# Two score banks lent to the last burst, a last row block in three pieces, and one hash a unit earlier

## The chip, the core and the metric

The kernel runs on one core of one Trainium2 chip. The core has a matrix engine (TensorE; PE in the profile, PEld for its weight loads), VectorE (DVE), ScalarE (ACT), GpSimd (POOL) and a sync engine (SP) that only issues transfers. The metric is the device time of one execution in microseconds, lower is better. A profiled execution gives a span, from the first to the last instruction, and a time that is a little longer.

## What is computed

Hash attention over 4 batches, 8 heads, 768 positions and 64 dimensions, and behind it a feed-forward block with a maximum of three projections. Attention is kept only between positions whose six hash bits agree:

```python
q_bits = (np.einsum('bhsd,dk->bhsk', q, proj) > 0)
k_bits = (np.einsum('bhsd,dk->bhsk', k, proj) > 0)
mask = q_bucket[:, :, :, None] == k_bucket[:, :, None, :]
scores = np.where(mask, scale * q @ k.T, -1e9)
attn = softmax(scores)                  # 768 x 768 for each head
x = (attn @ v) laid out as (3072, 512)
h = np.maximum(np.maximum(x @ w1, x @ w2), x @ w3)   # 3072 x 768
out = h @ w_out                                      # 3072 x 512, float32
```

## The kernel before, in words

**Scores and hash in one matmul.** For each head there is a tile S with the 64 transposed dimensions of q and k in rows 0 to 63 and the hash bits, as plus and minus one half, in the rows below. One matmul over these rows gives the score and the agreement of the bits at once; the exponential's bias takes away what disagreeing bits leave. Heads are handled in pairs for batch 0 and in quads (four heads, numbered 0 to 7) after it. A quad's q and k are loaded by POOL or SP (`load_quad`), transposed on VectorE (`turn`, L200), narrowed to bf16 on POOL (`narrow`, L205), and placed into S by eight SP transfers (`place`, L210). `quad_hash` (L219) makes the bits: sixteen matmuls into a bank, a comparison on VectorE (L222) and four SP transfers into S (L230): first the key's two halves, then the query's. The transfers are sent one unit after the matmuls.

**Units.** Queries are cut into nine chunks: three of 256 queries for batch 0, then six of 384. A unit is one chunk, one head and a part of the keys: its scores (L296, two or three matmuls) go into a score tile of two PSUM banks; ScalarE takes the exponential (L304) into one of 24 buffers. There are 192 units. The score pool holds two such tiles, so four banks of PSUM are its own. In unit u TensorE first computes the scores of unit u + 1, then the jobs listed for that unit (`when`), then one group of FFN work if any stands in the list, then a burst if one is due, then a hash if `hash_at` names one. All engines follow the order in which this Python program writes the instructions; transfers on SP, ACT and POOL each keep their order too.

**Adds and bursts.** From the fourth chunk on VectorE adds the exponentials of a head (L327, L330). When four heads of a chunk are done, a burst follows: `sums` (L351, matmuls with ones), with a chain on VectorE that turns them into reciprocals (L358 to L362), then `values` for side 0 and for side 1 (L373, 24 matmuls each), whose results VectorE scales into x (L380). The 32-column matmuls of a burst and of a hash work in four strips of the array.

**Banks.** The other four PSUM banks are a ring: `bank()` takes the one that has been free longest, `give()` puts it back in the program's order. Hash, sums, values and FFN groups all draw from it, and a group waits until the engine that empties its bank has done so.

**FFN.** For each chunk 18 groups of four matmuls (L406) make the three projections; the first goes to SBUF by ScalarE or VectorE (L411, L413), the other two are merged in by VectorE (L415). Then for each block of 128 rows two items of three matmuls with w_out (L450), a copy on ScalarE (L454) and a transfer to the output (L456). The groups of a chunk join a list two units after its last burst, and about one is taken from the list in each unit. After unit 191 the last three listed groups, the last burst, what is left of chunk 7's list and the whole FFN of chunk 8 follow. The very last block of 128 rows of chunk 8 is special: `last` (L427) computes it in two pieces of 256 columns (L431), copied by ScalarE (L435) and VectorE (L437) and sent from ACT's and SP's queue (L439).

Of the kernel before, what the change touches and what calls it, by code (L numbers as in the profile page):

```python
# [17 lines left out]
def kernel(  # L18
# [73 lines left out]
        return i, bank_tiles[i]  # L92

    def give(i):
        free_banks.append(i)


    nat, t32, t16, s_of, where, v_at = {}, {}, {}, {}, {}, {}
# [240 lines left out]
    def burst(c, i):  # L339
        b, q0, w = chunks[c]  # L340
        held = {}
        rb = []

        def sums(m0, m1):
            if m0 == 0:
                held["s"] = bank()
            sm = held["s"][1]
            bs = [sum_blocks(c, 4 * i + x) for x in range(4)]
            for m in range(len(bs[0])):
                for x in range(4):  # L350
                    nc.tensor.matmul(sm[Q * x : Q * (x + 1), 0:w], ones[:, :], bs[x][m],  # L351
                                     start=(m == 0), stop=(m == len(bs[0]) - 1))
            if m1 == NM:
                ys = ys_pool.tile([P, HALF], FP32, tag="ys", name="ys")
                rr = small.tile([P, HALF // Q], FP32, tag="rr", name="rr")
                n = w // Q
                rb.append(rb_pool.tile([P, HALF], FP32, tag="rb", name="rb"))
                nc.vector.transpose(ys[:, 0:w], sm[:, 0:w])  # L358
                give(held["s"][0])
                nc.vector.tensor_scalar(out=rr[:, 0:n], in0=ys[:, 0:w:Q], scalar1=EPS * S, scalar2=None, op0=AluOp.add)  # L360
                nc.vector.reciprocal(rr[:, 0:n], rr[:, 0:n])
                nc.vector.transpose(rb[0][:, 0:w], rr[:, 0:n].unsqueeze(2).to_broadcast((P, n, Q)))  # L362

        def values(side, m0, m1):
            if m0 == 0:
                held[side] = bank()
            av = held[side][1]
            first = (b, i, side) not in sv_of
            n = w + 1 if first else w
            for m in range(m0, m1):  # L370
                cb = block_of(b, m)
                for x in range(4):
                    nc.tensor.matmul(av[Q * x : Q * (x + 1), 0:n], v_at[2 * b + i][:, x, cb * D + side : (cb + 1) * D : 2],  # L373
                                     weights_of(c, 4 * i + x, m)[:, 0:n], start=(m == 0), stop=(m == NM - 1))
            if m1 == NM:
                if first:
                    sv_of[b, i, side] = small.tile([P, 1], FP32, tag=f"sv{side}", name="sv")
                    nc.vector.tensor_scalar(out=sv_of[b, i, side][:], in0=av[:, w : w + 1], scalar1=EPS, scalar2=None,
                                            op0=AluOp.mult)
                nc.vector.scalar_tensor_tensor(out=xt_of(c)[:, 2 * i + side, 0:w], in0=av[:, 0:w],  # L380
                                               scalar=sv_of[b, i, side][:], in1=rb[0][:, 0:w], op0=AluOp.add, op1=AluOp.mult)
                give(held[side][0])
                if side == 1:
                    for h in range(4 * i, 4 * i + 4):
                        for n in range(parts_of(c)):
                            a = at_of[unit_at[c, h, n]]
                            if b == 0 and i == 1:
                                nc.gpsimd.memset(blocks(at_tiles[a], HALF)[:, :, HALF : HALF + 2], 1.0)
                                at_form[a] = HALF
                            at_free.append(a)  # L390

        return sums, values


    def ffn_groups(c):
        b, q0, w = chunks[c]
        xt = xt_of(c)
        hts, gs, l2 = {}, [], {}
        jobs = [(fb, wi) for fb in range(NFB) for wi in range(3)]
        if c == 0:  # L400
            jobs = [(fb, wi) for wi in range(3) for fb in range(NFB)]
        for fb, wi in jobs:
            def go(fb=fb, wi=wi):
                k_, ps = bank()
                for jc in range(NJC):
                    nc.tensor.matmul(ps[:, 0:w], w_sb[wi][:, jc, fb * P : (fb + 1) * P], xt[:, jc, 0:w],  # L406
                                     start=(jc == 0), stop=(jc == NJC - 1))
                if wi == 0:
                    hts[fb] = h_pool.tile([P, HALF], FP16, tag="ht", name="ht")
                    if w == HALF:  # L410
                        nc.scalar.copy(hts[fb][:, 0:w], ps[:, 0:w])  # L411
                    else:
                        nc.vector.tensor_copy(hts[fb][:, 0:w], ps[:, 0:w])  # L413
                else:
                    nc.vector.tensor_tensor(out=hts[fb][:, 0:w], in0=hts[fb][:, 0:w], in1=ps[:, 0:w], op=AluOp.max)  # L415
                give(k_)
            gs.append(go)
        rows = out[b * S : (b + 1) * S, :].rearrange("(p c) m -> c p m", c=NM)

        def out_rows(tb):  # L420
            if c < NCH - 1:
                return o_pool.tile([P, DM], FP32, tag="osb", name="osb")
            if "end" not in nat:
                nat["end"] = nat_pool.tile([P, 4 * NM * D], FP32, tag="nat", name="nat")
            return nat["end"][:, tb * DM : (tb + 1) * DM]

        def last(part, tb):  # L427
            k_, ps = bank()
            cs = slice(part * DM // 2, (part + 1) * DM // 2)
            for fb in range(NFB):  # L430
                nc.tensor.matmul(ps[:, 0 : DM // 2], hts[fb][:, tb * P : (tb + 1) * P], wout_sb[:, fb, cs],  # L431
                                 start=(fb == 0), stop=(fb == NFB - 1))
            osb = out_rows(tb)
            if part == 0:
                nc.scalar.copy(osb[:, cs], ps[:, 0 : DM // 2])  # L435
            else:
                nc.vector.tensor_copy(osb[:, cs], ps[:, 0 : DM // 2])  # L437
            give(k_)
            (nc.scalar, nc.sync)[part].dma_start(rows[block_of(b, q0 // P + tb)][:, cs], osb[:, cs])  # L439

        def item(tb, part):
            def go2(part, tb=tb):
                if c == NCH - 1 and tb == w // P - 1:
                    last(part, tb)
                    return
                if part == 0:
                    l2[tb] = bank()
                k_, ps = l2[tb]
                for fb in range(part * MH, (part + 1) * MH):
                    nc.tensor.matmul(ps[:, 0:DM], hts[fb][:, tb * P : (tb + 1) * P], wout_sb[:, fb, :],  # L450
                                     start=(fb == 0), stop=(fb == NFB - 1))
                if part == 1:
                    osb = out_rows(tb)
                    nc.scalar.copy(osb[:, 0:DM], ps[:, 0:DM])  # L454
                    give(k_)
                    nc.sync.dma_start(rows[block_of(b, q0 // P + tb)], osb[:, 0:DM])  # L456
            gs.append(lambda: go2(part))

        ntb = w // P
        steps = [(0, 0)]  # L460
        for tb in range(1, ntb):
            steps += [(tb, 0), (tb - 1, 1)]
        steps.append((ntb - 1, 1))
        if c == NCH - 1:
            steps = steps[:-3] + [steps[-2], steps[-3], steps[-1]]
        for tb, part in steps:
            item(tb, part)
        return gs
# [6 lines left out]
    with tc.manual_schedule():  # L475
# [88 lines left out]
        for g in range(2, NQUAD):  # L564
            b2, i2 = divmod(g, 2)
            need = UPB * b2 + 12 * i2
            for n, side in enumerate((1, 0)):
                name = (side, g)
                if g > 3:
                    us = [SPREAD[b2][0] + SPREAD[b2][1] * (8 * i2 + 4 * n + n2) // 4 for n2 in range(4)]  # L570
                    for x in range(4):
                        when(us[0] - 14 + x, load_quad, side, g, (x,), nc.gpsimd)
                else:
                    us = [need - {2: 26, 3: 23}[g] + 4 * n + n2 for n2 in range(4)]
                for n2, u2 in enumerate(us):
                    when(u2, turn, name, n2 // 2, n2 % 2)
                    if n2 % 2:
                        when(u2 + 1, narrow, name, n2 // 2)
                when(us[3] + 3, place, name, range(4))
            hash_at[{2: 32, 3: 48, 4: need - 12}.get(g, need - 9)] = g  # L580
            when({2: 36, 3: 46}.get(g, need - 22), load_v, g)

        ffn, credit = [], 0
# [75 lines left out]
```

## Time and profile before

| what | value |
|---|---|
| median of 3 runs | 268.19 us (267.94 to 268.28) |
| the profiled execution | 268.58 us |
| its span | 266.6 us |
| TensorE busy | 257.9 us, 97% of the span |
| VectorE busy | 208.9 us, 78% |
| ScalarE busy | 177.3 us, 67% |
| GpSimd busy | 69.9 us, 26% |
| granted TensorE clock | full speed throughout |

Rows of the timeline give the start and the length of a run of equal instructions, the engine, the source line, the operation, the tile written and read, the shape and the count; in brackets the idle time before it and who ended it. Matmuls are pipelined, so the length of a row holds the drain of its last matmul, and starts are the better measure. "PEld" is a weight load, "SPq" the issue of a transfer. A row of busy time by stretch gives, for PE, PEld, DVE, ACT and POOL, busy microseconds and instructions, then the granted clock, the share of the 16 DMA engines and the GB/s. Rows of groups end in busy time, mean ns of one, and idle time before.

### The profile page before, as it was taken

The numbers are of one execution on the slowest core, as the hardware profiler recorded it, in microseconds if no ns is written. First come the engines' busy times: TensorE is split into PE (matmuls) and PEld (weight loads), VectorE is DVE, ScalarE is ACT, GpSimd is POOL, SyncE is SP. The second block draws the span as 40 slices with busy tenths as digits, with TensorE's granted clock in tenths as the row PEclk, the third lists the DMA queues.
The fourth block names the chain that finished last, engine by engine and source line by source line (L and its number), as shares of the span: only waits on it lengthen the run. The fifth ranks groups of instructions, "written<-read, shape, count | busy, mean of one in ns | idle before, by whom it ended". The sixth has DMA issues, their size and how long they took to land.

```text
span 266.6 us, 6482 instructions
## 1 busy us (share of the span) xinstructions
PE 257.9 (97%) x2505; PEld 154.4 (58%) x2505; DVE 208.9 (78%) x493; ACT 177.3 (67%) x257; POOL 69.9 (26%) x132
## 2 busy tenths in 40 slices
PE   7899999999799999999999999999999999999995
PEld 4555557885566575555555554555555555554552
DVE  2897685987499999978998997899849785888361
ACT  3596785676758694984869578484895859581322
POOL 3588652355032535240141612011000000000000
PEclk9999999999999999999999999999999999999999
DMA  6977999969703791982054472802030003000303
GB/s 203 316 156 135 230 234 212 245 114 233 185 22 86 159 231 18 234 222 53 4 167 131 56 182 43 204 8 61 15 118 4 0 2 119 2 0 2 118 0 118
DMA packets 20717, 30.95 MB, mean 116 GB/s; under 512 B 2608, under 2 KB 15248, under 8 KB 20688
## 3 DMA queue, kind: packets, MB, share of 16 engines
q0 software_dynamic: 8128, 13.37, 26.6%
q1 hardware_dynamic: 12128, 16.66, 21.8%
q10 hardware_dynamic: 432, 0.52, 0.6%
q8 instruction: 19, 0.31, 0.5%
q14 instruction: 10, 0.08, 0.1%
HBM read 25.17 MB, written 6.29 MB: 118 GB/s over the span
## 4 chain that ended last, share of the span: by engine, by line
PE 84%; DVE 7%; ACT 5%; issue 3%; DVEq 0%; ACTq 0%
PE ms L406 31%; PE sc L296 21%; PE ms L373 11%; PE ms L450 10%; ACT AT L304 4%; PE ms L351 3%; PE ms L219 3%; DVE ht L415 2%; DVE ad L327 1%; PE ms L498 1%; PE ms L122 1%; PE ms L149 1%; DVE T L131 1%; PE ms L169 1%; DVE S L174 1%
## 5 line engine op out<-in xcount | busy, mean ns | idle before, releaser
L304 ACT ACTIVATE AT<-sc 128x768 f16<-128x768 f32 x192 | 152.3, 816 | 62.2 <-PE sc L296 60.7
L406 PE MATMUL ms<-xT,w_sb 128*128 128x384 f16 (+1 forms) x648 | 114.8, 307 | 0.1
L296 PE MATMUL sc<-S 72*128 72x384 bf16 (+1 forms) x432 | 93.6, 308 | 3.3 <-ACT AT L304 1.8
L406 PEld LDWEIGHTS <-w_sb 128*128 128x128 f16 x648 | 62.7, 97 | 35.9 <-issue 0.4
L415 DVE TENSOR_TENSOR ht<-ht,ms 128x384 f16<-128x384 f16 (+1 forms) x108 | 54.3, 504 | 24.4 <-PE ms L406 13.4
L296 PEld LDWEIGHTS <-S 72*128 72x128 bf16 (+1 forms) x432 | 39.4, 98 | 35.7 <-issue 15.5
L205 POOL TENSOR_SCALAR T<-T 128x768 bf16<-128x768 f32 x24 | 22.8, 952 | 95.4 <-issue 50.5
L450 PE MATMUL ms<-wout_sb,ht 128*128 128x512 f16 x138 | 35.5, 378 | 0.0
L373 PE MATMUL ms<-AT,vo 128*32 128x385 f16 (+3 forms) x864 | 35.2, 309 | 0.3 <-DVE ht L415 0.3
L327 DVE TENSOR_TENSOR ad<-ad,AT 128x768 f16<-128x768 f16 x48 | 26.6, 553 | 2.1 <-ACT AT L304 1.3
L373 PEld LDWEIGHTS <-vo 128*32 128x32 f16 x864 | 22.6, 96 | 9.6 <-issue 1.8
L200 DVE STREAM_TRANSPOSE T<-nat 128x384 f32<-128x384 f32 x48 | 27.0, 565 | 0.2 <-DMA nat<-in_q_dram 0.2
L327 DVE TENSOR_TENSOR ad<-AT,AT 128x768 f16<-128x768 f16 x48 | 26.2, 546 | 0.2 <-ACT AT L304 0.2
L411 ACT CAST ht<-ms 128x384 f16<-128x384 f32 x36 | 17.3, 479 | 8.1 <-PE ms L406 8.1
L380 DVE SCALAR_TENSOR_TENSOR xT<-ms,sv,rb 128x384 f16<-128x384 f32 (+1 forms) x36 | 19.8, 567 | 1.4
L450 PEld LDWEIGHTS <-ht 128*128 128x128 f16 x138 | 13.3, 97 | 13.0 <-issue 0.3
L454 ACT COPY osb<-ms 128x512 f32<-128x512 f32 x21 | 12.2, 585 | 8.2 <-PE ms L450 6.3
L330 DVE TENSOR_TENSOR ad<-ad 128x384 f16<-128x384 f16 x32 | 15.5, 484 | 1.1
L136 POOL TENSOR_SCALAR S<-T 64x384 bf16<-64x384 f32 (+1 forms) x23 | 14.2, 617 | 5.0 <-DVE T L131 3.5
L358 DVE STREAM_TRANSPOSE ys<-ms 128x384 f32<-128x384 f32 (+1 forms) x18 | 9.6, 532 | 6.2 <-PE ms L351 6.2
L194 POOL DMA_DIRECT2D nat<-in_q_dram x20 | 11.1, 560 | 0.1
L413 DVE CAST ht<-ms 128x256 f16<-128x256 f32 x18 | 7.4, 413 | 4.0 <-PE ms L406 3.9
(48 smaller groups left out, 123.0 us busy)
## 6 DMA issues: line engine op xcount, KB each, us to landing
out_dram<-osb SPq DMA_DIRECT2D x21, 256.0 KB
S<-T SPq DMA_DIRECT2D x48, 96.0 KB
nat<-in_q_dram POOLq DMA_DIRECT2D x20, 192.0 KB, 6.7
vo<-in_v_dram POOLq DMA_DIRECT2D x8, 384.0 KB, 6.2
nat<-in_k_dram POOLq DMA_DIRECT2D x16, 192.0 KB, 5.7
w_sb<-in_moe_w_dram POOLq DMA_DIRECT2D x3, 768.0 KB, 6.9
nat<-in_k_dram SPq DMA_DIRECT2D x10, 192.0 KB
nat<-in_k_dram SPq DMA_DIRECT2D x3, 384.0 KB
```

Source lines behind the costliest of these rows:

```text
L200: nc.vector.transpose(t32[name][:, u, half * HALF : (half + 1) * HALF], i_)
L205: nc.gpsimd.tensor_scalar(out=t16[name][:, u, :], in0=t32[name][:, u, :], scalar1=RS, scalar2=1.0, op0=AluOp.mult, op1=AluOp.mult)
L296: nc.tensor.matmul(views[j], s_of[kn][0 : D + bits, kx, m * P : (m + 1) * P], s_of[qn][0 : D + bits, qx, q0 : q0 + w], start=True, stop=True)
L304: nc.scalar.activation(t[:, :, 0:w], whole, ActFn.Exp, bias=-SCALE * 0.25 * bits, scale=SCALE)
L327: nc.vector.tensor_tensor(out=sum_of[c, h][:], in0=t[0], in1=t[n], op=AluOp.add)
L330: nc.vector.tensor_tensor(out=t[:, 0, :], in0=t[:, 0, :], in1=t[:, 1, :], op=AluOp.add)
L373: nc.tensor.matmul(av[Q * x : Q * (x + 1), 0:n], v_at[2 * b + i][:, x, cb * D + side : (cb + 1) * D : 2], weights_of(c, 4 * i + x, m)[:, 0 ...
L380: nc.vector.scalar_tensor_tensor(out=xt_of(c)[:, 2 * i + side, 0:w], in0=av[:, 0:w], scalar=sv_of[b, i, side][:], in1=rb[0][:, 0:w], op0=A ...
L406: nc.tensor.matmul(ps[:, 0:w], w_sb[wi][:, jc, fb * P : (fb + 1) * P], xt[:, jc, 0:w], start=(jc == 0), stop=(jc == NJC - 1))
L411: nc.scalar.copy(hts[fb][:, 0:w], ps[:, 0:w])
L415: nc.vector.tensor_tensor(out=hts[fb][:, 0:w], in0=hts[fb][:, 0:w], in1=ps[:, 0:w], op=AluOp.max)
L450: nc.tensor.matmul(ps[:, 0:DM], hts[fb][:, tb * P : (tb + 1) * P], wout_sb[:, fb, :], start=(fb == 0), stop=(fb == NFB - 1))
```

## The change

Three things change.

- In the second burst of the last chunk, `sums` and `values` for side 0 take a tile of the score pool in place of a bank of the ring; `values` for side 1 still takes a bank of the ring. `give` passes over what was not taken from the ring.
- The last block of 128 rows is computed in three pieces of columns, 256, 128 and 128. The first is copied by VectorE and sent from SP's queue, the second by ScalarE from its own queue, the third by VectorE from SP's queue.
- The hash of quad 3 stands at unit 47 in place of 48: ahead of the last burst of chunk 2 in place of behind it.

```diff
     def give(i):
-        free_banks.append(i)
+        if i is not None:
+            free_banks.append(i)
...
+        def own_bank(key):
+            if c == NCH - 1 and i == 1 and key != 1:
+                return None, sc_ps.tile([P, 2, 512], FP32, tag="sc", name="sc")[:, 0, :]
+            return bank()
+
         def sums(m0, m1):
             if m0 == 0:
-                held["s"] = bank()
+                held["s"] = own_bank("s")
...
         def values(side, m0, m1):
             if m0 == 0:
-                held[side] = bank()
+                held[side] = own_bank(side)
...
-        def last(part, tb):
+        def last(tb, cs, use_act):
             k_, ps = bank()
-            cs = slice(part * DM // 2, (part + 1) * DM // 2)
+            n = cs.stop - cs.start
             for fb in range(NFB):
-                nc.tensor.matmul(ps[:, 0 : DM // 2], hts[fb][:, tb * P : (tb + 1) * P], wout_sb[:, fb, cs],
+                nc.tensor.matmul(ps[:, 0:n], hts[fb][:, tb * P : (tb + 1) * P], wout_sb[:, fb, cs],
                                  start=(fb == 0), stop=(fb == NFB - 1))
             osb = out_rows(tb)
-            if part == 0:
-                nc.scalar.copy(osb[:, cs], ps[:, 0 : DM // 2])
+            if use_act:
+                nc.scalar.copy(osb[:, cs], ps[:, 0:n])
             else:
-                nc.vector.tensor_copy(osb[:, cs], ps[:, 0 : DM // 2])
+                nc.vector.tensor_copy(osb[:, cs], ps[:, 0:n])
             give(k_)
-            (nc.scalar, nc.sync)[part].dma_start(rows[block_of(b, q0 // P + tb)][:, cs], osb[:, cs])
+            (nc.scalar if use_act else nc.sync).dma_start(rows[block_of(b, q0 // P + tb)][:, cs], osb[:, cs])
...
-                    last(part, tb)
+                    if part == 0:
+                        last(tb, slice(0, DM // 2), False)
+                    else:
+                        last(tb, slice(DM // 2, 3 * DM // 4), True)
+                        last(tb, slice(3 * DM // 4, DM), False)
                     return
...
-            hash_at[{2: 32, 3: 48, 4: need - 12}.get(g, need - 9)] = g
+            hash_at[{2: 32, 3: 47, 4: need - 12}.get(g, need - 9)] = g
```

## The prediction

> **What bounds the kernel now.** I read the page first, then TensorE's rows in order of time, looking for places where its starts fall out of their pitch, and only there the queues and the other engines.
>
> ```profile
> span 266.6 us, 6482 instructions
> PE 257.9 (97%) x2505; PEld 154.4 (58%) x2505; DVE 208.9 (78%) x493; ACT 177.3 (67%) x257; POOL 69.9 (26%) x132
> ```
>
> TensorE is busy for 97% of the span, so time is to be had only where it stops, and after its last matmul. I found two odd stops after the opening. The first (timeline of TensorE, of SyncE's queue, busy time by stretch, DMA queues from 66 to 71 us):
>
> ```profile
> 68.78 0.48 PE L296 MATMUL sc<-S 72*128 72x384 bf16 x2
> 69.54 0.49 PE L296 MATMUL sc<-S 72*128 72x384 bf16 x2
> 71.95 0.48 PE L296 MATMUL sc<-S 72*128 72x384 bf16 x2 [1.48 <-ACT AT L304]
> ...
> 53.29 6.18 SPq L210 DMA_DIRECT2D S<-T  x8
> 62.08 2.94 SPq L230 DMA_DIRECT2D S<-bits  x4
> 63.63 0.67 SPq L230 DMA_DIRECT2D S<-bits  x1
> ...
> 70.00:71.00 1.00, 0.47 (x5) 0.18 (x2) 1.00 (x3) 0.94 (x2) 0.00 (x0) 1.00 1.01 270
> 71.00:72.00 1.00, 0.05 (x1) 0.08 (x2) 0.03 (x1) 0.00 (x0) 0.00 (x0) 1.00 0.56 213
> ...
> q0 software_dynamic: 250, 0.74, 69.9%
> q1 hardware_dynamic: 318, 0.40, 31.9%
> ```
>
> Scores come every 0.76 us (68.78, 69.54); the next should start at 70.30 and starts at 71.95, so **1.65 us** are lost. ScalarE is named, but in the stretch 71 to 72 it is busy 0.00: it had long been done. Counting scores back to the first of 72 rows and 384 columns (unit 48), the late one is unit 60, the first to read the S tile of quad 3. The last things written into that tile are the hash bits, sent in four transfers at 62.08 to 65.02. Key and query, first halves, are the first and third of them; the third is issued at 63.63, and the wait ends 8.3 us later. In between the DMA engines are full (share 1.01), most of it POOL's loads on queue 0 (69.9% against 31.9% for SyncE's queue 1). So I read the stop as the third transfer of bits coming late. The landing itself has no row; it is inferred.
>
> The second stop is in the last burst, shown below with its terms.
>
> **The change, part by part: the hash.** Quad 3's hash is moved from the end of unit 48, behind the burst of chunk 2, to the end of unit 47, ahead of it. Its 16 matmuls, the copy of the bits and the four transfers move; their number stays.
>
> ```profile
> 48.77 0.49 PE L296 MATMUL sc<-S 70*128 70x256 bf16 x3
> 51.72 0.50 PE L296 MATMUL sc<-S 70*128 70x256 bf16 x3
> ...
> 55.17 0.56 DVE L200 STREAM_TRANSPOSE T<-nat 128x384 f32<-128x384 f32 x1
> 57.10 0.49 PE L296 MATMUL sc<-S 72*128 72x384 bf16 x2
> 59.95 1.46 PE L219 MATMUL ms<-T,pj 128*32 128x384 f32 x16
> 61.35 0.50 PE L296 MATMUL sc<-S 72*128 72x384 bf16 x2
> 61.49 0.56 DVE L222 TENSOR_SCALAR bits<-ms 128x384 bf16<-128x384 f32 x1 [0.28 <-PE ms L219]
> ...
> 99.01 0.49 PE L296 MATMUL sc<-S 72*128 72x384 bf16 x2
> 101.30 0.50 PE L296 MATMUL sc<-S 72*128 72x384 bf16 x2
> ...
> 61.09 1.09 POOL L194 DMA_DIRECT2D nat<-in_k_dram  x2 [0.40 <-issue]
> nat<-in_k_dram POOLq DMA_DIRECT2D x4, 192.0 KB, 6.2
> 74.05 0.57 DVE L200 STREAM_TRANSPOSE T<-nat 128x384 f32<-128x384 f32 x1
> ```
>
> What the move costs TensorE: from scores to scores, less the pitch of 0.76, burst and hash together take 61.35 - 57.10 - 0.76 = 3.49. A burst alone takes 51.72 - 48.77 - 0.76 = 2.19, a hash alone 101.30 - 99.01 - 0.76 = 1.53. Apart they cost 3.72: **+0.23 us**, an entry to and an exit from the 32-column matmuls more.
>
> What it gives: the hash starts at about 57.2 (where unit 49's scores start now, plus the entry) instead of 59.95. Its last input, the transpose of 55.17, is done. The copy follows 61.49 - 59.95 = 1.54 later, from 58.74 to 59.30. SyncE's queue has the eight placements ahead of it until 53.29 + 6.18 = 59.47, so the bits go out from 59.5: 2.6 us earlier, in the same order. TensorE reaches unit 60 at 70.30 + 0.23 = 70.53. The third transfer, if its time in the queue stays, lands at 71.95 - 2.6 = 69.4. The stop goes if 71.95 - 70.53 = 1.42 of the 2.6 come through. The bounds: all of the stop goes, -1.65 + 0.23 = -1.42; nothing comes through, 0 (TensorE then only arrives later at the same landing). I take **-1.42**, because the four transfers stand in one queue behind the same placements, only sooner.
>
> Who is late next: the burst is 1.5 us later, and behind its matmuls wait POOL's memsets and, queued after those, the two key loads of 61.09 and four query loads. The key loads land 6.2 after issue, the last near 67.8, then near 69.3; VectorE transposes them first at 74.05, then 72.6. It holds. Chunk 2's x is later by as much, but its FFN groups stand behind all of chunk 1's in a list that gives about one a unit. In VectorE's queue the copy moves ahead of the burst's chain, which then has a matmul burst to wait for anyway. ScalarE starves in two short pauses instead of one.
>
> **The last burst.** Sums and the first value matmuls get a score bank each instead of a bank of the four.
>
> ```profile
> 229.93 0.35 PE L351 MATMUL ms<-ad,ones 128*32 128x384 f16 x4
> 230.11 2.12 PE L373 MATMUL ms<-AT,vo 128*32 128x384 f16 x48
> ...
> 239.22 0.81 ACT L304 ACTIVATE AT<-sc 128x768 f16<-128x768 f32 x1 [0.17 <-PE sc L296]
> 241.78 1.21 DVE L415 TENSOR_TENSOR ht<-ht,ms 128x384 f16<-128x384 f16 x2
> 242.38 0.35 PE L351 MATMUL ms<-ad,ones 128*32 128x384 f16 x4
> 243.04 2.13 PE L373 MATMUL ms<-AT,vo 128*32 128x384 f16 x48 [0.31 <-DVE ht L415]
> 244.67 1.17 DVE L380 SCALAR_TENSOR_TENSOR xT<-ms,sv,rb 128x384 f16<-128x384 f32 x2
> 247.70 4.55 PE L406 MATMUL ms<-xT,w_sb 128*128 128x384 f16 x27
> ```
>
> In the burst before, values follow sums by 0.18 us; here by 0.66, because the values' bank is emptied by the second of the two L415 that end at 242.99. With a score bank they follow by 0.18: **-0.48 us**. The new wait is on the exponential that last read the score bank; that ends at 240.03, before the sums' adds. The second values still take a ring bank, the one of the first L415, free before they start. VectorE's chain of the burst is not shortened: x is finished at 245.84 as now. That was hidden under projections until 247.70 and, with TensorE 0.48 earlier, still has 1.4 us of cover. Had those projections not stood between, the gain would be nothing. It cannot be a loss, since a bank is only added; 0 and -0.6 are its bounds.
>
> **The last row block.** Its 512 columns come as 256, 128 and 128 instead of 256 and 256; copies on VectorE, ScalarE, VectorE.
>
> ```profile
> 261.99 1.47 PE L431 MATMUL ms<-wout_sb,ht 128*128 128x256 f16 x12
> L431 PEld LDWEIGHTS <-ht 128*128 128x128 f16 x12 | 1.2, 98 | 0.3
> 9.09 1.48 PE L122 MATMUL ms<-iden,nat 128*128 128x128 f32 x12
> L122 PEld LDWEIGHTS ms<-iden,nat 128*128 128x128 f32 x48 | 6.0, 148 | 0.4 <-issue 0.2
> ...
> 263.50 0.42 DVE L437 COPY nat<-ms 128x256 f32<-128x256 f32 x1 [3.27 <-PE ms L431]
> 263.96 0.33 SPq L439 DMA_DIRECT2D out_dram<-nat  x1
> ...
> 264.80:265.20 0.40, 0.00 (x0) 0.00 (x0) 0.00 (x0) 0.00 (x0) 0.00 (x0) 1.00 0.94 318
> 265.20:265.60 0.40, 0.00 (x0) 0.00 (x0) 0.00 (x0) 0.00 (x0) 0.00 (x0) 1.00 0.07 21
> ```
>
> Twelve matmuls of 256 columns took 1.47 with the last one's drain, a pitch of about 0.11; the last six become twelve of 128. If columns set the pitch, it is half, and nothing changes; if each has to sit out its weight load of 98 ns, twelve cost 1.18 instead of 0.66, +0.52. The nearest row has the same 128 by 128 shape in f32: pitch about 0.11 while its loads show 148 ns, so a pitch may run 0.04 or so below the load's length. I take 0.06 to 0.07, **+0.14**. The last copy: 384 columns took 0.56 (the bits), 256 took 0.42, so 128 take 0.28: **-0.14**. Issue is unchanged (the first copy and its transfer moved to VectorE and SyncE come before, off the end; ScalarE's middle piece has its own queue). The last transfer is half as large, but the DMA engines run full (0.94) until 265.2 on the same bytes, now in more rows: **-0.10**, between -0.2 and 0. Sum -0.10, bounds -0.2 and +0.4.
>
> A sentence apart: the Trainium skill, "TensorE: Matmul & The Clock Gate", section "Back-to-back issue gap", gives about 81 ns per pair of load and matmul at 128 columns; by that, an estimate, the twelve take 0.97, +0.32, and the total would be 0.18 worse than mine. No row of this kernel shows the f16 case.
>
> **Sum.** -1.42 - 0.48 - 0.10 = -2.00. The profiled execution took 268.58, 0.39 above the median of 268.19 (span 266.6): 266.58 there, **266.2** as a median.
>
> **The rivals.**
> - *The bits come no earlier.* If the transfers are held not by when they are issued but by POOL's loads, they land when those thin out, near 71 us, as now. For it: queue 0's 69.9%. Against: queue 1 moved 0.40 MB in the same time. Then -0.48 - 0.10: 267.6. Chance 0.14. (The Trainium skill, "DMA: Bandwidth & Descriptors", "Queues, rings and completion order", says that each engine takes turns between queues packet by packet; by it queue 1 is slowed but served, and the shares above agree.)
> - *VectorE paces the stretch after.* If it was catching up behind the stop, the 1.42 comes back as bank waits: 267.6. Against: it also idled in the stop (0.03 busy from 71 to 72), so both start the stretch drained either way. Chance 0.04.
> - *Narrow matmuls pay their whole load.* +0.52 - 0.14 instead of -0.10: 266.7. Chance 0.08.
> - *Slower: the last small rows.* B and C write 512-byte rows. If such rows travelled like the bits (768-byte rows, 8.3 us from issue to the end of the wait) instead of the 1.3 us in which the last piece's data now moves (263.96 to about 265.3), up to 7 us would be added; the sign turns once it is over 2.0. Against: the bits shared the engines with loads, and at the end there are none. At its full price 273. Chance 0.04.
>
> My forecast as it stands has 0.70, with its own range 265.8 to 266.6. From 265.7 to 267.8 all but the slower case and some of the edges is held. A difference of 0.2% (0.54 us) is about what can be told from none here. The cases at 267.6 lie on that bound and are halved: faster 0.87, same 0.09, slower 0.04.
>
> **What would show it.** Right: the L219 group of quad 3 near 57.2 and its bits issued near 59.5; unit 60's scores 0.76 after unit 59's; about 0.23 more between unit 48 and unit 50; L373 0.18 after L351 in the last burst; twelve narrow matmuls at a pitch of 60 to 70 ns; the last copy 0.28. Wrong: a stop at unit 60 that still ends near 72, new bank waits between 80 and 110 us, or a last transfer that ends later after its issue than now.

## The result, and the profile after

The changed kernel takes 267.14 us (median of 5 runs, 267.10 to 267.48) against 268.28 for the kernel before beside it (267.94 to 268.88): ratio 0.9958, 95% interval 0.9943 to 0.9973. That is faster by 1.1 us, a little over half of the 2.0 that I forecast. It lies outside my forecast's own range (265.8 to 266.6) and inside the wide one (265.7 to 267.8), which was to hold the rivals too, all but the slower one. The profiled execution takes 267.30 us with a span of 265.3 (before: 268.58 and 266.6).

```profile
span 265.3 us, 6498 instructions
PE 258.3 (97%) x2511; PEld 154.6 (58%) x2511; DVE 209.1 (79%) x494; ACT 177.4 (67%) x257; POOL 70.1 (26%) x132
```

These are the rows of the changed kernel's timeline that answer to the ones shown of before: TensorE and SyncE's queue around the moved hash (L220, sent by L231) and unit 60, then the last burst and the last row block. Line numbers are 1 to 10 higher than before.

```profile
57.66 1.50 PE L220 MATMUL ms<-T,pj 128*32 128x384 f32 x16
59.09 0.50 PE L297 MATMUL sc<-S 72*128 72x384 bf16 x2
59.81 2.94 SPq L231 DMA_DIRECT2D S<-bits  x4
62.05 0.50 PE L297 MATMUL sc<-S 72*128 72x384 bf16 x2
...
70.25 0.49 PE L297 MATMUL sc<-S 72*128 72x384 bf16 x2
71.02 0.49 PE L297 MATMUL sc<-S 72*128 72x384 bf16 x2
...
142.29 0.49 PE L297 MATMUL sc<-S 72*128 72x384 bf16 x2
...
241.16 0.35 PE L357 MATMUL sc<-ad,ones 128*32 128x384 f16 x4
241.33 1.15 PE L379 MATMUL sc<-AT,vo 128*32 128x384 f16 x24
243.38 2.76 PE L460 MATMUL ms<-wout_sb,ht 128*128 128x512 f16 x12
260.28 1.49 PE L437 MATMUL ms<-wout_sb,ht 128*128 128x256 f16 x18
```

Unit 60 (71.02) now follows unit 59 (70.25) at the ordinary pitch: the stop of 1.65 us is gone. The landing of the bits, which no row of the views shows, can be read from the semaphore updates that the trace keeps: the third transfer landed at 71.86 before, 0.09 ahead of unit 60, and at 68.66 after. The values (241.33) follow the sums (241.16) by 0.17. Two rows of before that are needed for what follows:

```profile
143.50 0.48 PE L296 MATMUL sc<-S 72*128 72x384 bf16 x2
245.10 1.25 PE L450 MATMUL ms<-wout_sb,ht 128*128 128x512 f16 x5
```

Going down the two traces, the shift against before is as follows. The first scores start at 8.56 instead of 8.08, +0.48, in code that did not change. Unit 50 is at 62.05 instead of 61.35, +0.70: the opening, and 0.22 for the split. Unit 60 is at 71.02 instead of 71.95, -0.93. The scores that stood at 143.50 before are at 142.29, -1.21: a small stop there has gone too, which I had not looked at. The w_out matmuls behind the burst are at 243.38 instead of 245.10, -1.72, and the last block begins at 260.28 instead of 261.99, -1.71. But the span ends only 1.3 us earlier: 0.45 us are lost in the last five us, nearly all of it behind TensorE's last work.

The profiled time falls by 1.28, and the opening alone was 0.48 longer; the first scores of the executions profiled here start anywhere from 7.64 to 8.65 us in code that is the same. Their rows, of before, of after, and of the two extremes among the experiments (the hash alone; the loads moved):

```profile
8.08 0.49 PE L296 MATMUL sc<-S 70*128 70x256 bf16 x3 [0.60 <-DVE S L174]
8.56 0.49 PE L297 MATMUL sc<-S 70*128 70x256 bf16 x3 [0.70 <-DVE S L175]
7.64 0.49 PE L296 MATMUL sc<-S 70*128 70x256 bf16 x3 [0.60 <-DVE S L174]
8.65 0.49 PE L296 MATMUL sc<-S 70*128 70x256 bf16 x3 [0.75 <-DVE S L174]
```

With openings 1.0 us apart, the spans of two executions can't settle half a microsecond, so below I use distances inside a trace and the medians of runs.

The end, in rows of the source line of the closing code (SyncE's part of it), of SyncE's waits, and of the groups of the last block, first before, then after. SyncE first waits there for the semaphores of the transfers, and the first DRAIN instruction stands behind the last of these waits:

```profile
L654 SPq DRAIN  x3: 7/7/13, 265.7 to 266.1; - x3
SPq L654 <- DMA out_dram<-nat: 0.9, 3, 0.4
```

```profile
L664 SPq DRAIN  x3: 7/7/13, 264.5 to 264.8; - x3
SPq L664 <- DMA out_dram<-nat: 1.4, 1, 1.4
...
L437 PE MATMUL ms<-wout_sb,ht 128*128 128x128 f16 x12 | 0.8, 219 | 0.0
261.87 0.29 DVE L443 COPY nat<-ms 128x128 f32<-128x128 f32 x1 [0.32 <-PE ms L437]
262.19 0.33 SPq L445 DMA_DIRECT2D out_dram<-nat  x1
```

The narrow matmuls cost next to nothing: by their starts in the trace their pitch is 0.056, half of the 0.109 of the wide ones, and the block takes 1.49 instead of 1.47 in all. The last copy took 0.29, as reckoned, but it starts 1.59 behind the block's first matmul instead of 1.51. Yet SyncE's first closing drain comes 265.7 - 261.99 = 3.7 us after the block's first matmul before and 264.5 - 260.28 = 4.2 after. Before, SyncE waited for three landings in turn, the longest 0.4; now it waits 1.4 for one that it asks about early, and comes to the rest, long landed, after that. The trace's semaphore updates put the last landing 3.67 us after the block's first matmul before and 3.70 after: the data is there at the same time, and the way out is longer. From the block's first matmul to the end of the span, called the end below, it is 4.60 us before and 5.06 after.

### The profile page after: what moved, and what is told of

The parts are those of the page before. It is cut to its first block, busy times and chain, and to the rows that moved or that the text cites. A ratio compares the mean times of both kernels' runs of the same rounds, so it can differ in the third digit from the quotient of the medians.

```text
span 265.3 us, 6498 instructions
## 1 busy us (share of the span) xinstructions
PE 258.3 (97%) x2511; PEld 154.6 (58%) x2511; DVE 209.1 (79%) x494; ACT 177.4 (67%) x257; POOL 70.1 (26%) x132
## 4 chain that ended last, share of the span: by engine, by line
PE 88%; DVE 5%; ACT 3%; issue 2%; DVEq 0%; ACTq 0%
PE ms L412 33%; PE sc L297 22%; PE ms L460 11%; PE ms L379 10%; ACT AT L305 3%; PE ms L220 3%; PE ms L357 3%; PE ms L123 1%; PE ms L508 1%; PE ms L150 1%; DVE ht L421 1%; DVE ad L328 1%; DVE S L175 1%; PE ms L170 1%; DVE T L132 1%
## 5 line engine op out<-in xcount | busy, mean ns | idle before, releaser
L379 PE MATMUL ms<-AT,vo 128*32 128x385 f16 (+3 forms) x840 | 34.2, 308 | 0.0
L386 DVE SCALAR_TENSOR_TENSOR xT<-ms,sv,rb 128x384 f16<-128x384 f32 (+1 forms) x35 | 19.2, 565 | 1.3
L175 DVE TENSOR_SCALAR S<-ms 6x384 bf16<-6x384 f32 x16 | 8.9, 554 | 2.5 <-PE ms L170 2.2
```

## The experiments

My theory after the result: the stop at unit 60 was late bits, and the hash gives 1.4; the banks give 0.5; the three pieces cost about 0.45, because one more transfer shifts the eight semaphores that the transfers of SP and ACT use in turn (128 transfers in the trace before, 129 after). The last transfer then counts on the one that the closing waits ask early, and the others are asked one by one behind it. The rivals: the pieces or their small rows cost it; the stop went because something else shifted; the gap in the burst moved somewhere else.

**Each part alone, and without the third part** (four kernels, compared on one chip). Hash alone:

```diff
-            hash_at[{2: 32, 3: 48, 4: need - 12}.get(g, need - 9)] = g
+            hash_at[{2: 32, 3: 47, 4: need - 12}.get(g, need - 9)] = g
```

> The kernel before with the hash of quad 3 at unit 47 alone. If the stop at unit 60 was the third transfer of bits landing late, the stop of 1.65 us is gone and the split costs 0.23: ratio near 0.995 (-1.4 us). If the bits land when the loads on queue 0 thin out, unit 60 still starts near 72 us and the ratio is 1.000. The end, from the last block's first matmul to the end of the span, stays at 4.6 us.

Measured: ratio 0.9948, interval 0.9931 to 0.9964 (267.03 against 268.37 us). TensorE's timeline of this kernel around unit 60:

```profile
69.87 0.49 PE L296 MATMUL sc<-S 72*128 72x384 bf16 x2
70.64 0.49 PE L296 MATMUL sc<-S 72*128 72x384 bf16 x2
```

No stop; the hash alone gives 1.3 us between the medians, the forecast's 1.4.

The score banks alone (`own_bank` and the new `give`, nothing else):

```diff
-                held["s"] = bank()
+                held["s"] = own_bank("s")
...
-                held[side] = bank()
+                held[side] = own_bank(side)
```

> The kernel before with the two score banks for the last burst alone. By the forecast the values follow the sums by 0.18 us instead of 0.66 and all behind them moves by -0.5 us: ratio near 0.998. If the gain is given back where VectorE's chain or the output copies wait, the ratio is 1.000 although the gap is gone.

Measured: ratio 0.9998, interval 0.9976 to 1.002, which says nothing either way for half a microsecond. The profile says why. These are rows of TensorE, SyncE's queue and ScalarE near 143 us, then the last burst:

```profile
142.54 0.49 PE L297 MATMUL sc<-S 72*128 72x384 bf16 x2
144.96 0.48 PE L297 MATMUL sc<-S 72*128 72x384 bf16 x2 [1.27 <-ACT AT L305]
136.56 0.34 SPq L462 DMA_DIRECT2D out_dram<-osb  x1
137.00 3.89 SPq L211 DMA_DIRECT2D S<-T  x4
143.22 0.58 ACT L460 COPY osb<-ms 128x512 f32<-128x512 f32 x1 [1.73 <-DMA out_dram<-osb]
...
243.83 0.35 PE L357 MATMUL sc<-ad,ones 128*32 128x384 f16 x4
244.00 1.15 PE L379 MATMUL sc<-AT,vo 128*32 128x384 f16 x24
```

The gap in the burst is gone (0.17), but a third stop, of 1.4 us here, stands at 144.96: the scores wait for ScalarE, which waits with an output copy (143.22) until an earlier output transfer has left its row buffer; there are two. The same place cost 0.29 us in the profile before and nothing after the change. It differs from execution to execution, and can hide the half microsecond.

The three pieces alone (the new `last` and its calls, hash at 48, no score banks for the burst):

```diff
-                    last(part, tb)
+                    if part == 0:
+                        last(tb, slice(0, DM // 2), False)
+                    else:
+                        last(tb, slice(DM // 2, 3 * DM // 4), True)
+                        last(tb, slice(3 * DM // 4, DM), False)
```

> The kernel before with the last row block in three pieces alone. My forecast of the tail was -0.1 us. In the changed kernel's profile the last transfer ends 3.70 us after the block's first matmul, as before (3.68), but it counts on another semaphore, which stands early in the list that the closing waits go through one by one; if these waits make the difference, this kernel is 0.4 us slower than before (ratio 1.0016), with its end 5.0 us behind the block's first matmul. If the small rows or something else made the changed kernel lose, the end differs from that, or the last landing does.

Measured: slower, ratio 1.0024, interval 1.0005 to 1.0042. The last block and SyncE's closing drains in its trace:

```profile
261.80 1.49 PE L432 MATMUL ms<-wout_sb,ht 128*128 128x256 f16 x18
L659 SPq DRAIN  x3: 7/7/13, 266.0 to 266.3; - x3
```

266.0 - 261.80 = 4.2, as in the whole change: the third part costs what the end showed.

Hash and banks, with the last block left in two pieces (the first two diffs together):

> The changed kernel without its third part: hash at 47 and score banks, last block in two pieces as before. If the three pieces cost 0.4 us, the gain is 1.4 + 0.5 = 1.9 us, ratio near 0.993, against 0.9958 for the whole change. If the three pieces cost nothing, the ratio is 0.996.

Measured: ratio 0.9941, interval 0.9918 to 0.9964 (266.42 us). The last block and SyncE's closing drains:

```profile
259.75 1.47 PE L437 MATMUL ms<-wout_sb,ht 128*128 128x256 f16 x12
L660 SPq DRAIN  x3: 7/7/13, 263.5 to 263.8; - x3
```

263.5 - 259.75 = 3.8, and its end is 4.60 us. Its median lies 0.6 us under that of the hash alone, but the two intervals overlap, so the times don't show the banks' half microsecond. The traces do: from the first matmul of the last burst's sums to the last block's first matmul it is 19.61 to 19.62 us in all four executions without the score banks (before, the hash alone, the pieces alone, the loads moved) and 19.12 in all eight with them. The 0.50 is won in the burst and not given back before TensorE's last block.

**Is it the pieces or the order of the waits?** Two kernels, one from each side, each executed once, under the profiler (266.75 and 266.51 us), so only distances inside their traces count. First the whole change with one transfer fewer in the turn:

```diff
-            when(u, load_quad, side, g, range(4), nc.sync)
+            when(u, load_quad, side, g, range(3), nc.sync)
+            when(u, load_quad, side, g, (3,), nc.gpsimd if side == 0 else nc.sync)
```

> The whole change, with one of the four loads of quad 3's queries moved from SP's queue to POOL's. That is one transfer fewer on the eight semaphores that the SP and ACT queues take in turn, so the last output transfer counts on the one that the closing waits ask last. If the order of those waits is the cause, the end from the last block's first matmul goes from 5.06 back to 4.60 us, with three pieces of columns still. If the pieces themselves cost it, it stays at 5.05.

Then hash and banks with two pieces, and one transfer more, at the start:

```diff
-        load_pair(3, nc.sync)
+        load_pair(3, nc.sync, (1,))
+        load_pair(3, nc.sync, (0,), 0, 1)
+        load_pair(3, nc.sync, (0,), 1, 2)
```

> Hash at 47 and score banks with the last block in two pieces as before, and one load at the start split into two transfers, so that the last output transfer counts on the semaphore that is asked early. By the order of the closing waits the end goes from 4.60 to 5.05 us though the last block is untouched; if the pieces are the cause it stays at 4.60.

The second, with two pieces; rows of TensorE, the closing drains and SyncE's waits:

```profile
259.36 1.47 PE L437 MATMUL ms<-wout_sb,ht 128*128 128x256 f16 x12
L662 SPq DRAIN  x3: 7/7/13, 263.6 to 263.9; - x3
SPq L662 <- DMA out_dram<-nat: 1.3, 1, 1.3
```

263.6 - 259.36 = 4.2 with an untouched last block, and one long wait again: its end went from 4.60 to 5.04 us, because of one more transfer at the start of the program. From the other side, three pieces with the turn shifted back:

```profile
259.93 1.49 PE L437 MATMUL ms<-wout_sb,ht 128*128 128x256 f16 x18
L665 SPq DRAIN  x3: 7/7/12, 263.7 to 264.0; - x3
SPq L665 <- DMA out_dram<-nat: 0.9, 2, 0.5
```

The block began at 259.93, so the first drain is back at 3.8. The closing waits are thus shown as the cause. The other traces agree: in the seven further executions whose last transfer counts on the semaphore asked last, with two pieces of columns, the end is 4.60 to 4.61 us, and in the four where it counts on the one asked early, one of them with two pieces, 5.04 to 5.07. With three pieces and the turn shifted back the whole end fell only to 4.94, though, not to 4.60: the last step of the closing code, behind the drains, took 0.34 longer in this one execution. In its trace 0.31 of that lie on GpSimd, between its last DRAIN and its next semaphore instruction. Why is open.

**Was it the loads that held the bits?** The kernel before, hash at 48, eight query loads on the other queue:

```diff
-                        when(us[0] - 14 + x, load_quad, side, g, (x,), nc.gpsimd)
+                        eng = nc.sync if side == 0 and g < 6 else nc.gpsimd
+                        when(us[0] - 14 + x, load_quad, side, g, (x,), eng)
```

> The kernel before, hash still at 48, with the four query loads of quad 4 and the four of quad 5 moved from POOL's queue to SP's, where those of quad 4 come behind the bits (eight more, so the turn of semaphores at the end is the same). If the bits were late because POOL's loads shared the engines with them, they land earlier, the stop at unit 60 (1.65 us) goes or shrinks below 0.5 with the hash where it was, and the ratio is near 0.994. If it is only the time of issue that counts, the stop stays near 1.6 us and the ratio is 1.000.

Measured: ratio 0.994, interval 0.992 to 0.996 (266.65 us), as much as the hash alone, with the hash where it was. SyncE's queue, TensorE and the queues' shares from 66 to 71 us:

```profile
62.64 3.16 SPq L230 DMA_DIRECT2D S<-bits  x4
69.03 1.99 SPq L194 DMA_DIRECT2D nat<-in_q_dram  x4
...
70.11 0.49 PE L296 MATMUL sc<-S 72*128 72x384 bf16 x2
70.87 0.49 PE L296 MATMUL sc<-S 72*128 72x384 bf16 x2
...
q1 hardware_dynamic: 539, 0.76, 52.7%
q0 software_dynamic: 40, 0.08, 8.9%
```

The bits go out as late as before (62.64, in an execution that opened 0.57 later), yet unit 60 at 70.87 does not stop. With the query loads behind them instead of beside them (queue 0 at 8.9% instead of 69.9%), they land in time. So lateness had two legs, and either cures it: send the bits sooner, or take the loads off the engines meanwhile. The semaphore updates give the third transfer's time from issue to landing: 8.0 to 8.2 us in the three executions with the hash at 48 and POOL's query loads beside the bits, 6.2 to 7.3 with the hash at 47, where the bits are sent before these loads are issued, and 5.0 with the loads moved (landed at 69.41, 1.46 ahead of unit 60). That fits the rule of the Trainium skill ("DMA: Bandwidth & Descriptors", "Queues, rings and completion order") that engines take turns between queues: a small transfer is slowed by what the other queue holds, not shut out.

**The third stop.** Hash and banks, with three output row buffers:

```diff
-    h_pool = ctx.enter_context(tc.tile_pool(name="hpool", bufs=8))
-    o_pool = ctx.enter_context(tc.tile_pool(name="opool", bufs=2))
+    h_pool = ctx.enter_context(tc.tile_pool(name="hpool", bufs=6))
+    o_pool = ctx.enter_context(tc.tile_pool(name="opool", bufs=3))
```

> Hash at 47 and score banks with the last block as before, and three output row buffers in place of two (the FFN's h tiles are cut from eight to six to make room). The stop near 143 us (0.29 in the profile before, 1.44 in the one with the banks alone, none in the whole change) stands behind a copy that waits for an output transfer; with a third buffer it should never be there, so the time is 0 to 0.5 us below hash and banks (ratio 0.992 to 0.994) and the spread between runs is smaller. If the copy did not wait for the buffer, nothing changes.

Measured: ratio 0.9934, interval 0.9913 to 0.9955 (266.04 to 267.11 us); no stop near 143 in its trace. Against hash and banks (0.9941) the ratio doesn't settle it: the stop comes and goes there too, and the one execution profiled had none.

**A kernel for each cause, and the whole change again.** Score banks, three row buffers and the query loads on SP's queue, hash at 48, last block in two pieces:

> Hash at 48 with the query loads of quads 4 and 5 on SP's queue, score banks, three output row buffers and the last block in two pieces: each cause as the runs so far name it, without the 0.23 us that the hash costs apart from the burst. By the sum 268.4 - 1.65 - 0.5 - 0.3 to 0.6 (the third stop) gives 265.7 to 266.0, ratio near 0.991; if the pieces overlap or the loads on SP's queue cost elsewhere, it is no faster than hash and banks, 0.994.

> The whole change once more, beside the one above on the same chip: ratio 0.996 as before, 0.4 us above what hash and banks gave (0.994) if the order of the closing waits costs that, and an end of 5.05 us again; if 5.06 was one execution's accident, the end is 4.60.

Measured on one chip: 266.06 us, ratio 0.991, interval 0.9883 to 0.9937, against 267.09, ratio 0.995, interval 0.993 to 0.997, for the whole change, whose end was 5.07 us again. Rows of TensorE in the first, at unit 60, near 142 us, and in the last burst:

```profile
69.50 0.49 PE L297 MATMUL sc<-S 72*128 72x384 bf16 x2
70.27 0.49 PE L297 MATMUL sc<-S 72*128 72x384 bf16 x2
...
141.53 0.49 PE L297 MATMUL sc<-S 72*128 72x384 bf16 x2
142.51 0.49 PE L297 MATMUL sc<-S 72*128 72x384 bf16 x2
...
240.40 0.35 PE L357 MATMUL sc<-ad,ones 128*32 128x384 f16 x4
240.57 1.15 PE L379 MATMUL sc<-AT,vo 128*32 128x384 f16 x24
```

All three stops are gone and the hash still shares its entry and exit with the burst. This version beats both kernels: 2.2 us below the one before, 1.0 below the change. Against hash and banks alone (0.9941) the intervals overlap.

## Why the prediction was right or wrong

- **The hash: right, in size and mechanism.** Forecast -1.42; in the trace the distance from unit 50 to unit 60 shrank by 1.63, the split cost 0.22, which makes -1.41, and alone it gave 1.3 between medians. It started at 57.66 with 0.48 of late opening, so 57.2, and the bits went out at 59.81, so 59.3, both about as reckoned. The third transfer landed at 68.66, so 68.2, a little sooner than the 69.4 that I reckoned. The rival by which the bits come no earlier fell with the first experiment; its premise, that POOL's loads hold the bits, was nevertheless true.
- **The last burst: right.** Forecast -0.48; between unit 60 and the w_out matmuls 0.79 was gained, 0.28 of it at the third stop, so 0.51 here; the same 0.50 separates all executions with the banks from all without, and the cover ahead of the projections held.
- **The last row block: wrong, and it is the step that failed.** The term was -0.10 with bounds -0.2 and +0.4. It measured +0.46, just outside, at the end of the trace (5.06 against 4.60) and 0.0024 of the time when alone, 0.6 us. Of the parts that I reckoned, the matmuls cost +0.02 by their rows and +0.08 up to the start of the last copy (forecast +0.14), and the copy gave -0.13 (forecast -0.14). The last transfer, for which I took -0.10, took 0.08 longer from issue to landing, though half as large (262.19 to 263.98, 1.79 us, against 263.96 to 265.67, 1.71): one of my own signs of being wrong, and I can't say which of its smaller rows, the third transfer beside it or chance did it. Together they make +0.03 where I had -0.10. The Trainium skill, "TensorE: Matmul & The Clock Gate", "Back-to-back issue gap", gives about 81 ns for a load and a matmul at 128 columns; the 56 ns measured here disagree. The larger part, +0.43, I left out, and it stands behind the landing: I ended the sum at the last transfer, and counted a new transfer as bytes and rows, not as a step in the turn of semaphores.
- **What is then left.** -1.41 - 0.51 + 0.46 = -1.46, ratio 0.9946, inside both intervals of the whole change (0.9943 to 0.9973 and 0.993 to 0.997). The stop near 143 us and the start of the first scores move from execution to execution by as much as the remainder; I ascribe nothing to it. That 267.14 lies in my wide range is in part luck: the range was stretched to there for rivals that did not occur, and the cost that did was in none of them.
- **The other rivals.** VectorE did not pace the stretch behind the stop: the 1.6 us gained at unit 60 is still there at 142. Narrow matmuls did not pay their loads (56 ns a matmul against loads of 98 ns), and rows of 512 bytes were not slowed like the bits: the last landing is 3.70 us behind the block's first matmul instead of 3.67. The slower rival did not occur, but the third part alone is slower, by another mechanism than the one I gave.

## What to carry to other kernels

When a kernel is 97% busy on one engine, list that engine's starts and look for those out of pitch; two of the three stops here carried ScalarE's name, and both were transfers that landed or left late. A late small transfer is cured by sending it sooner or by moving the bulk loads that share the engines, and the second leaves the compute order alone. Add a transfer anywhere and the last one may count on another semaphore: look at the distance from the last landing to the end of the span, and not at the last landing alone.

## What the runs showed of the hardware that I had not expected

- The closing code asks the transfers' semaphores one by one. With the last transfer on one asked early, the way from the block's first matmul to the first drain is 4.2 us, with it on the last about 3.8, in all twelve executions, whatever was changed to shift it.
- Twelve 128 by 128 f16 matmuls of 128 columns with a weight load each ran at a pitch of 0.056 us, although their loads show 98 ns each.
- The first scores start between 7.64 and 8.65 us in the profiled executions; these two extremes have the same code ahead of them.
